# A longer hold for urgent work in a static instruction plan, and a later start of the second half's attention

## The chip, the cores and the metric

One core of one Trainium2 chip. The metric is the device time of one execution in microseconds (us). A kernel is profiled in one execution and timed in several. Times are given as the median of the runs. A ratio is the mean time of one kernel's runs over the mean of the other's runs of the same rounds, so it is not quite the ratio of the medians that I quote.

## The reference, cut to what matters

```python
h  = x + A(_layernorm(x))          # A: x @ wqkv, phi = where(t>0, t+1, exp(t)) + 1e-6,
                                   #    linear attention (kv = phi(k)^T v, o = phi(q) kv / den), @ wo
h2 = h + B(_layernorm(h))          # B: relu(x @ W_gate) * (x @ W_up) @ W_down
# x is 1 x 2048 x 1024 bf16; 32 heads of 32; W_gate, W_up 1024 x 3584, W_down 3584 x 1024
```

Up to about 210 us the core works on A and on the two layernorms. The rest is B, a stream of large matmuls.

## The kernel before

The program is written as calls in a natural order. A `Plan` records each call as a node with an engine, a length (`hold`), a latency, its predecessors and a latest start (`late`). It then lists them once, at build time, in one fixed order for each engine, and issues that. So the order of every engine's queue is the plan's decision, made with the plan's idea of how long things take. The chip then follows the order whatever the true lengths are.

Some words for the calls. The large matmuls are done by 2 x 2 blocks with seven *products* in place of eight, so VectorE forms *sums* (or differences) of blocks of weights or of activations beforehand, and adds the products up afterwards. A *clamp* and a *join* make phi (min with 1, then max with 0 and add); a *residual add* adds x to a product; a *group* is a part of B's weights. In the views, `mem` is the on-chip memory SBUF, `psum` the one that TensorE's products land in, which the program divides into banks, and `tiny` is one or a few numbers per row.

The plan's lengths (cut):

```python
def cost(self, eng, op, out, ins, k):
    ...
    if eng == "vector":
        narrow = all(self.nbytes(a) == 2 and a.space != PSUM for a in (out, *ins) if self.free(a) > 1)
        mode = {"tensor_tensor": 2, "tensor_scalar": 4, "memset": 2}.get(op, 1) if narrow else 1
        ...
        return n / (0.96 * mode) + 69 + acc, 95 + self.SEM
    if eng == "scalar":
        return n / 1.2 + (51 if psum else 93) + 2 * acc, 105 + self.SEM
    return n * 1.15 + 100, 60 + self.SEM            # gpsimd
```

The choice of the next node (cut): of what is ready on the engine that is free first, the node with the earliest `late`. If a clearly more urgent node of that engine is ready within half of the chosen node's length, the engine holds for it.

```python
s, e, a = best                                      # time, engine, its available nodes
now = [i for i in a if nodes[i].ready <= s]
i = min(now, key=lambda i: (nodes[i].nom if e == "tensor" else nodes[i].late, i))
v = nodes[i]
if e != "tensor":
    soon = [j for j in a if s < nodes[j].ready < s + 0.5 * v.hold and nodes[j].late < v.late - 1500.0]
    if soon:
        i = min(soon, key=lambda j: (nodes[j].late, j))
        v = nodes[i]
        s = v.ready
v.start = s
clock[e] = s + v.hold
```

The normalise of a layernorm (x times 1/std minus mean) runs on GpSimd, and so does a tiny negation of the mean:

```python
def finish(self, on_dve=False):
    self.rstd_()                                    # two tiny ScalarE activations
    xn = self.xn
    (nc.vector if on_dve else nc.gpsimd).tensor_scalar(out=xn, in0=self.x, scalar1=self.negm[:], scalar2=self.rstd[:], ...)
    nc.sync.dma_start_transpose(out=XI[self.i][:, :, self.r:self.r + P], in_=xn)
```

The second half's attention (token blocks 8 to 15; `nd01`, `nd2` are numerator and denominator, then `wo`) is put into a queue of units, one of which is taken at each tick between matmul groups:

```python
t8, t9 = tiles[NTS:NTS + 2]
tick.units.extend([t8.nd01, None, t9.nd01, None, t8.nd2, t9.nd2] + steps(NTS, 2 * NTS, 2, 0, False)[4:])
```

## Time and profile before

| | before |
|---|---|
| median of 3 runs | 727.81 us (727.63 to 728.01) |
| profiled run | 726.09 us, span 724.3 us |
| TensorE busy | 99% of the span |
| VectorE, ScalarE, GpSimd busy | 78%, 38%, 11% |

TensorE is nearly always busy, so the kernel can only gain where TensorE pauses. In this document **a pause is the distance between the starts of two matmuls less the pace of the first** (215.6 ns for 512 columns), worked out from the start times in the trace. That is some 0.16 us more than the idle time that a timeline line shows, as the ends of matmuls overlap the next starts. The prediction shows the lines and how they are read.

### The profile page before, as it was taken

The numbers are of one execution on the slowest core, as the hardware profiler recorded it, in microseconds if no ns is written. First come the engines' busy times: TensorE is split into PE (matmuls) and PEld (weight loads), VectorE is DVE, ScalarE is ACT, GpSimd is POOL, SyncE is SP. The second block draws the span as 40 slices with busy tenths as digits, with TensorE's granted clock in tenths as the row PEclk, the third lists the DMA queues.
The fourth block names the chain that finished last, engine by engine and source line by source line (L and its number), as shares of the span: only waits on it lengthen the run. The fifth ranks groups of instructions, "written<-read, shape, count | busy, mean of one in ns | idle before, by whom it ended". The sixth has DMA issues, their size and how long they took to land.

```text
span 724.3 us, 11221 instructions
## 1 busy us (share of the span) xinstructions
PE 714.4 (99%) x4163; PEld 396.7 (55%) x4163; DVE 563.9 (78%) x954; ACT 277.3 (38%) x540; POOL 77.8 (11%) x88
## 2 busy tenths in 40 slices
PE   8999999999999999999999999999999999999998
PEld 4444545444444444444444444444444688888887
DVE  7897745887796885666767968769758879899996
ACT  5877555666554443333333333333333220001100
POOL 1342000002202110000000000000000004001452
PEclk9999999999999999999999999999999999999999
DMA  9556406069766630446145575685681878777974
GB/s 300 165 117 110 138 0 212 23 109 216 160 156 151 140 73 6 129 136 186 60 139 188 165 244 157 202 253 186 198 262 51 276 265 209 216 265 238 242 80 60
DMA packets 156503, 117.40 MB, mean 162 GB/s; under 512 B 54944, under 2 KB 140192, under 8 KB 156320
## 3 DMA queue, kind: packets, MB, share of 16 engines
q1 hardware_dynamic: 148832, 113.01, 53.9%
q0 software_dynamic: 7616, 3.67, 4.8%
q8 instruction: 32, 0.52, 0.3%
q14 instruction: 23, 0.19, 0.1%
HBM read 70.52 MB, written 34.08 MB: 144 GB/s over the span
## 4 chain that ended last, share of the span: by engine, by line
PE 85%; DVE 2%; DMA 2%; ACT 1%; issue 0%; POOL 0%; ACTq 0%
PE psum L122 85%; DVE mem L122 2%; DMA mem<-mem 2%; ACT mem L122 1%; POOL mem L122 0%; ACT tiny L122 0%; DVE tiny L122 0%; ACTq L122 0%
## 5 line engine op out<-in xcount | busy, mean ns | idle before, releaser
L122 PE MATMUL psum<-mem 128*128 128x512 f16 (+4 forms) x4147 | 713.3, 334 | 6.5 <-ACT mem L122 2.7
L122 PEld LDWEIGHTS <-mem 128*128 128x128 f16 (+1 forms) x4163 | 396.7, 98 | 323.8 <-issue 8.0
L122 DVE TENSOR_TENSOR mem<-psum,mem 128x512 f32<-128x512 f32 (+2 forms) x240 | 187.4, 794 | 99.3 <-ACT mem L122 65.1
L122 DVE TENSOR_TENSOR mem<-mem 128x512 f16<-128x512 bf16 (+8 forms) x400 | 241.6, 643 | 14.9 <-DMA mem<-mem 9.6
L122 ACT COPY mem<-psum 128x512 f32<-128x512 f32 (+2 forms) x124 | 92.7, 749 | 209.4 <-PE psum L122 197.9
L122 ACT COPY psum<-psum 128x512 f32<-128x512 f32 (+1 forms) x68 | 49.1, 722 | 160.3 <-PE psum L122 147.6
L122 POOL DMA_DIRECT2D out_dram<-mem x28 | 34.1, 1299 | 413.8 <-DVE mem L122 413.7
L122 ACT ACTIVATE mem<-psum 128x512 bf16<-128x512 f32 x90 | 53.6, 598 | 18.5 <-PE psum L122 18.0
L122 DVE SCALAR_TENSOR_TENSOR mem<-mem 128x512 bf16<-128x512 bf16 (+1 forms) x71 | 57.7, 813 | 1.3
L122 POOL TENSOR_SCALAR mem<-mem,tiny 128x1024 bf16<-128x1024 bf16 x28 | 37.5, 1338 | 196.9 <-ACT tiny L122 176.8
L122 DVE SCALAR_TENSOR_TENSOR mem<-psum,mem 128x512 bf16<-128x512 f32 x66 | 45.4, 688 | 11.9 <-PE psum L122 7.9
L122 ACT ACTIVATE mem<-mem,tiny 128x1024 bf16<-128x1024 bf16 x24 | 27.4, 1143 | 11.0 <-DVE tiny L122 5.8
L122 DVE TENSOR_SCALAR mem<-mem 128x512 bf16<-128x512 bf16 (+1 forms) x49 | 16.3, 332 | 17.6 <-ACT mem L122 17.4
L122 DVE TENSOR_TENSOR mem<-psum,tiny 128x384 bf16<-128x384 f32 (+1 forms) x48 | 22.9, 508 | 5.3 <-ACT tiny L122 3.9
L122 ACT ACTIVATE mem<-mem 128x1024 bf16<-128x1024 f32 (+1 forms) x23 | 24.3, 1056 | 6.5 <-DVE mem L122 6.4
L122 ACT ACTIVATE tiny<-tiny 128x1 f32<-128x1 f32 (+2 forms) x112 | 22.8, 206 | 7.5 <-DVE tiny L122 4.7
L122 ACT ACTIVATE tiny<-psum 128x12 f32<-128x12 f32 (+1 forms) x48 | 8.1, 169 | 13.9 <-PE psum L122 13.4
L122 DVE BATCH_NORM_STATS2 tiny<-mem 128x6 f32<-128x512 bf16 x16 | 10.2, 682 | 2.5 <-DMA mem<-in_A_x_dram 2.5
L122 ACT CAST mem<-psum 128x512 bf16<-128x512 f32 x18 | 10.4, 582 | 4.2 <-PE psum L122 3.7
L122 POOL TENSOR_SCALAR tiny<-tiny 128x1 f32<-128x1 f32 x14 | 4.7, 337 | 25.2 <-ACT mem L122 13.3
L122 ACT ACTIVATION_READ_ACCUMULATOR mem<-mem,tiny 128x1 f32 x24 | 4.5, 188 | 0.0
L122 DVE TENSOR_SCALAR tiny<-tiny 128x1 f32<-128x1 f32 x16 | 3.4, 210 | 0.3
(18 smaller groups left out, 14.4 us busy)
## 6 DMA issues: line engine op xcount, KB each, us to landing
l_dram<-mem SPq DMA_DIRECT2D x98, 128.0 KB, 2.2
mem<-l_dram SPq DMA_DIRECT2D x12, 896.0 KB, 6.4
mem<-in_A_x_dram SPq DMA_DIRECT2D x32, 256.0 KB, 3.0
mem<-in_B_W_up_dram SPq DMA_DIRECT2D x14, 512.0 KB, 5.3
mem<-in_B_W_gate_dram SPq DMA_DIRECT2D x14, 512.0 KB, 4.3
mem<-in_B_W_down_dram SPq DMA_DIRECT2D x28, 256.0 KB, 3.4
r_dram<-mem SPq DMA_DIRECT2D x56, 128.0 KB, 1.8
mem<-r_dram SPq DMA_DIRECT2D x8, 896.0 KB, 5.0
```

The source lines that it names most:

```text
L122: call = lambda: getattr(getattr(self.nc, eng), op)(*args, **k)
```

## The change

The intent: let the engines other than TensorE, VectorE and ScalarE above all, wait up to 1.2 lengths of the less urgent node, not 0.5, for an urgent one that is nearly ready, during the first 215 us of the plan, where TensorE's pauses are. And let the second half's attention start four ticks later, so that it meets the last projection less tightly.

```diff
+    SHORT = 215000.0
...
-                soon = [j for j in a if s < nodes[j].ready < s + 0.5 * v.hold and nodes[j].late < v.late - 1500.0]
+                wait = (1.2 if s < self.SHORT else 0.5) * v.hold
+                soon = [j for j in a if s < nodes[j].ready < s + wait and nodes[j].late < v.late - 1500.0]
...
-    tick.units.extend([t8.nd01, None, t9.nd01, None, t8.nd2, t9.nd2] + steps(NTS, 2 * NTS, 2, 0, False)[4:])
+    tick.units.extend([None] * 4 + [t8.nd01, None, t9.nd01, None, t8.nd2, t9.nd2] + steps(NTS, 2 * NTS, 2, 0, False)[4:])
```

## The prediction

> **What bounds the kernel now.** I read the page first, then the busy time of the engines by stretch, then each idle spot of TensorE in the timeline, and last the orders in which the two programs issue their instructions (an order has no times in it).
>
> ```profile
> PE 714.4 (99%) x4163; PEld 396.7 (55%) x4163; DVE 563.9 (78%) x954; ACT 277.3 (38%) x540; POOL 77.8 (11%) x88
> ```
>
> TensorE is busy for 99% of the span at full clock. Busy does not mean fast here, as matmul ends are modelled, so I checked the pace: from 300 to 400 us, a stretch of 128x512 matmuls, the table by stretch counts 465 in 100 us, 215 ns each. So after the attention the kernel is a full TensorE stream, and the change can only win what TensorE loses by waiting. Where it waits, by stretch (busy us and count of PE, PEld, DVE, ACT, POOL, then clock, DMA share, GB/s):
>
> ```profile
> 20.00:60.00 40.00, 38.83 (x203) 18.33 (x201) 34.40 (x68) 33.67 (x73) 16.76 (x19) 1.00 0.56 132
> 60.00:140.00 80.00, 79.65 (x437) 38.77 (x436) 52.07 (x89) 46.26 (x81) 3.94 (x5) 1.00 0.37 99
> 140.00:152.00 12.00, 11.16 (x67) 5.53 (x66) 11.76 (x24) 7.56 (x25) 0.00 (x0) 1.00 0.24 45
> 152.00:186.00 34.00, 34.00 (x190) 16.75 (x189) 26.16 (x66) 20.41 (x66) 8.71 (x7) 1.00 0.92 187
> 186.00:210.00 24.00, 21.82 (x117) 10.26 (x116) 20.62 (x41) 16.22 (x41) 1.36 (x2) 1.00 0.65 166
> 210.00:280.00 70.00, 70.00 (x355) 32.98 (x354) 55.09 (x113) 30.49 (x88) 9.81 (x8) 1.00 0.48 105
> 280.00:720.00 440.00, 440.00 (x2715) 265.48 (x2713) 348.40 (x532) 112.14 (x146) 34.07 (x28) 1.00 0.62 181
> ```
>
> Idle is 1.17 + 0.35 + 0.84 + 2.18 = 4.54 us, all before 210 us. An idle spot costs more than it shows: a 512-column matmul lasts 381 ns on average but starts follow at 215 ns, so a stream overlaps by 0.16 us that a pause loses too. From the matmul starts, the pauses of over 0.2 us sum to some 6.7 us. **That is the whole prize, 0.9% of 727.81 us**: 2% faster is out of reach.
>
> **What the Trainium skill says.** "VectorE: DVE Perf Modes", section "The TRN2 errata", gives 215 ns for an N=512 matmul; the trace agrees, so nothing is hidden in the busy stretches. "PSUM — Partial Sum Buffer", section "Engine vs sequencer instructions", says the ScalarE and VectorE queues are strict FIFO: an instruction that waits holds all behind it. The lines at 187.93 us below agree. "Perfetto Trace Analysis", section "Optimizing Scalar/DVE Operations", gives some 93 ns of overhead for ScalarE on SBUF and twice that for the profiled latency; the 128x1 activations here take 206 ns (page), while the kernel's plan books 1/1.2 + 93 = 94 ns. "DMA: Bandwidth & Descriptors", section "Two DMAs through the same engine are not ordered", says that descriptors of one queue start in order; no line of this trace shows that by itself, but I use it below for a transpose that changes places with a load.
>
> **The change part by part.** No work is added or removed: 4163 matmuls and the same instructions stand in both programs. (1) Before the plan's time of 215 us, VectorE and ScalarE may idle up to 1.2 (not 0.5) of an instruction's length for a more urgent one. (2) The second half's attention starts four units later. By the orders, VectorE has 368 of 921 entries at another place, ScalarE 189 of 507, and the TensorE order is the same up to 137 us. I followed each pause through the new order with durations of the old trace.
>
> Part one at 193 us, the largest pause. VectorE, then ScalarE:
>
> ```profile
> 187.93 0.42 DVE L122 TENSOR_TENSOR mem<-mem 128x512 f16<-128x512 bf16 x1 [2.76 <-DMA mem<-mem]
> 188.27 0.68 DVE L122 SCALAR_TENSOR_TENSOR mem<-psum,mem 128x512 bf16<-128x512 f32 x1
> ...
> 187.86 0.58 ACT L122 COPY mem<-psum 128x512 f32<-128x512 f32 x1 [2.99 <-PE psum L122]
> 189.60 1.06 ACT L122 ACTIVATE mem<-mem 128x1024 bf16<-128x1024 f32 x1 [1.15 <-DVE mem L122]
> 190.56 1.14 ACT L122 ACTIVATE mem<-mem,tiny 128x1024 bf16<-128x1024 bf16 x1
> ...
> 192.17 0.57 ACT L122 COPY mem<-psum 128x512 f32<-128x512 f32 x1
> ...
> 192.79 1.46 PE L122 MATMUL psum<-mem 128*128 128x512 bf16 x6 [1.46 <-ACT mem L122]
> ```
>
> A sum waits 2.76 us for a transpose and holds up the residual add behind it (its product was done at 186.1); the add then sets the start of two 1.1 us activations, and those stand before the copy that TensorE waits for (its input was ready at 190.4). In the new order the residual add comes before the sum, the long exp after the copy: add 186.1 to 186.8, its mean to 187.0, the square 188.45 to 189.6, two tiny ones to 190.0, an exp of 0.58 to 190.55, the copy to 191.1. TensorE gets there at 191.1. **-1.6 us.**
>
> At 147 to 151 us the chain of waits is a transpose of 3.12 us:
>
> ```profile
> 147.48 3.12 DMA mem<-mem
> 150.59 0.05 issue
> 150.64 1.47 PE psum L122 x6
> ```
>
> In the new order a 0.68 us sum no longer stands before the last product join, nor a 0.28 us clamp before the scaling that feeds the transpose. The transpose is issued 0.2 + 0.28 earlier, and two pauses of 0.2 just before shrink. **-0.5 us**; the transpose itself stays.
>
> At 29 and 55 us, in the opening:
>
> ```profile
> 20.50 6.22 DVE L122 TENSOR_TENSOR mem<-mem 128x512 f16<-128x512 bf16 x8 [0.37 <-DMA mem<-mem]
> ...
> 26.64 1.28 DVE L122 BATCH_NORM_STATS2 tiny<-mem 128x6 f32<-128x512 bf16 x2
> ...
> 28.02 0.69 DVE L122 TENSOR_TENSOR mem<-psum,mem 128x512 f32<-128x512 f32 x1
> ...
> 28.76 2.53 PE L122 MATMUL psum<-mem 128*128 128x512 bf16 x11 [0.54 <-DVE mem L122]
> ```
>
> TensorE waits (0.70 with the overlap) for the add at 28.02, which stood behind 1.28 us of statistics. The new order moves the statistics behind it. But it also lets VectorE hold, from about 18.1, for the transpose that landed at 20.48, and does one weight difference (1.22 us) and a clamp and join (1.0) after that wait, not before. So -1.28 + 2.2: about 0.9 us later. One relief: SyncE now issues that transpose before a 256 KB load, so it may land up to 0.9 us earlier (an estimate: 256 KB at the 303 GB/s of the first 20 us), but that load, which ScalarE needs at 20.2, then comes later. I take **+0.5 us** here. At 55 us (0.73 lost) the copy stood behind two tiny activations waiting for statistics; the new order puts them elsewhere: **-0.5**. At 68 us two more tiny activations of 0.2 come before the copy: +0.2. At 76 us an add passes a 1.22 us join: -0.2. The pause of 0.3 at 128 us has the same order in both: 0.
>
> Part two, 200 to 209 us: pauses of 0.72, 0.28 and 0.24 us, where attention pieces meet the ends of the last projection. Their matmuls now stand six to seven products of 0.86 us later, so the join they wait for is done. But the same vector work (3 scalings, joins, sums; DVE is busy 20.6 of 24 us) then meets the next products, and I find new waits of 0.1 to 0.7 us when I follow it. **-0.4.** The last transposes of that attention end some 3.5 us later; the first matmul that needs them comes 16 us after (263.0 against 279.0), so nothing is lost there.
>
> Sum: -1.6 - 0.5 + 0.5 - 0.5 + 0.2 - 0.2 - 0.4 = **-2.5 us**, 725.3 us.
>
> **The rivals.** (a) *Holding costs more than it saves*: the plan's times are too short (94 ns for 206; a transpose that lands 5.2 us after issue at 15.25 us, where it books 3.6), so holds last longer than meant. For it: VectorE is at 34.4 of 40 us from 20 to 60. Against it: only the hold at 18 us is near a pause; the later background work has 7 us and more to spare (a sum's end to its first matmul). If the opening loses 1.0 and the 55 us pause stays: 726.5 to 727.5. (b) *The stall only moves*: at 193 us TensorE comes earlier to the same congested vector work, and the gain is given back by 209 us: 726.5. (c) *Everything clears*: opening -0.7, all pauses to 209 gone: -6 us, 722. It would need the plan to be exact; the 3.1 us transpose alone forbids it.
>
> **Range and chances.** All three lie within 6 us. I predict 725.3 us, 723.3 to 727.6 at 8 in 10; wider upward, as (a) and (b) can come together. Faster by 2% would be 713.3, more than all pauses; slower by 2% needs 14.6 us of new ones. So within 2% is nearly sure.
>
> **What would show it.** Right: PE idle from 186 to 200 falls from about 1.5 to near 0 with VectorE no longer idle for a DMA at 185 to 188; 140 to 152 keeps one DMA pause of 0.3 to 0.6; 280 to 720 stays full with equal counts; the pause at 28.8 stays or grows, with a VectorE idle of 1.5 to 2.4 us just before 20.5. Wrong: no VectorE idle there and no pause at 29 (then nearer 724), or new PE pauses of over 1 us between 195 and 215 or in 210 to 280 (then 727 and more).

## The result, and the profile after

| | before | after |
|---|---|---|
| median of 5 runs each | 727.81 us (727.06 to 728.07) | 726.63 us (726.26 to 726.87) |
| ratio | | 0.9987 (95% interval 0.9973 to 1.0000) |
| profiled run | 726.09 us | 726.87 us |

The change gained about 1.2 us, 0.13%: the same within 2%. The interval ends at no gain (1.0000), and that of the repeat below just beyond it (1.0005); but none of the ten timed runs of the changed kernel (at most 727.02 us) is as slow as the fastest of the 14 runs of before in their rounds (727.04). The two *profiled* runs stand the other way round. The profile of before is the fastest of all its runs, the profile of after one of the slowest of the changed kernel. So before reading a difference into the two traces I needed to know which pauses belong to the order and which to the run.

The page of the changed kernel, engines and the GpSimd normalise (columns of the second line: count, busy us, mean ns, idle before and its cause):

```profile
PE 711.2 (98%) x4112; PEld 396.7 (55%) x4163; DVE 566.3 (78%) x954; ACT 277.3 (38%) x540; POOL 81.6 (11%) x88
...
L123 POOL TENSOR_SCALAR mem<-mem,tiny 128x1024 bf16<-128x1024 bf16 x28 | 40.8, 1459 | 181.7 <-ACT tiny L123 168.9
```

TensorE's row has 4112 of 4163 matmuls: 51 records are missing, so its busy time is too low, and the table by stretch below can't be set against that of before. All weight loads are there, and from them I filled in the starts. The second line is the first hint: the same 28 normalises took 1459 ns on average. Before, the row said:

```profile
L122 POOL TENSOR_SCALAR mem<-mem,tiny 128x1024 bf16<-128x1024 bf16 x28 | 37.5, 1338 | 196.9 <-ACT tiny L122 176.8
```

The changed kernel's busy time by stretch (PE, PEld, DVE, ACT, POOL, then clock, DMA share, GB/s):

```profile
20.00:60.00 40.00, 36.49 (x189) 17.45 (x192) 32.61 (x58) 30.45 (x67) 16.69 (x16) 1.00 0.49 120
...
140.00:152.00 12.00, 11.60 (x69) 5.76 (x68) 11.05 (x21) 8.97 (x27) 0.00 (x0) 1.00 0.12 23
152.00:186.00 34.00, 32.80 (x178) 16.08 (x183) 29.45 (x69) 18.77 (x63) 7.18 (x6) 1.00 0.86 180
186.00:210.00 24.00, 23.66 (x119) 11.07 (x120) 20.70 (x42) 16.49 (x38) 2.39 (x2) 1.00 0.75 173
```

186 to 210 us is now nearly full. 20 to 60 us lost 3.5 us of busy time (before: 1.2), and 152 to 186 us, full before, now has holes. Some of that is missing records, but the pauses say the same. Sums of TensorE's pauses in us by stretch; the second profile of each kernel comes from the experiments:

| stretch, us | before, 1st profile | before, 2nd | after, 1st | after, 2nd |
|---|---|---|---|---|
| 0 to 20 | 2.91 | 3.47 | 3.67 | 3.04 |
| 20 to 40 | 0.74 | 0.59 | 1.62 | 1.67 |
| 40 to 60 | 1.10 | 2.00 | 2.07 | 2.11 |
| 60 to 80 | 0.74 | 1.26 | 0.18 | 0.18 |
| 120 to 160 | 1.78 | 1.80 | 1.31 | 1.30 |
| 160 to 180 | 0.05 | 0.05 | 1.28 | 1.27 |
| 180 to 220 | 3.03 | 3.59 | 0.72 | 0.76 |
| 240 to 280 | 0.00 | 0.00 | 0.22 | 0.22 |

The stretch that the change was made for is mended. The timeline of the changed kernel there, VectorE, then ScalarE, then TensorE:

```profile
188.94 0.69 DVE L123 SCALAR_TENSOR_TENSOR mem<-psum,mem 128x512 bf16<-128x512 f32 x1 [0.89 <-PE psum L123]
...
190.71 1.55 DVE L123 TENSOR_TENSOR mem<-mem 128x512 f16<-128x512 bf16 x4 [0.21 <-DMA mem<-mem]
...
190.67 0.59 ACT L123 COPY mem<-psum 128x512 f32<-128x512 f32 x1 [2.59 <-PE psum L123]
191.15 1.15 ACT L123 ACTIVATE mem<-mem,tiny 128x1024 bf16<-128x1024 bf16 x1
...
193.26 0.59 ACT L123 COPY mem<-psum 128x512 f32<-128x512 f32 x1
...
185.72 22.29 PE L123 MATMUL psum<-mem 128*128 128x512 bf16 x110
208.24 4.00 PE L123 MATMUL psum<-mem 128*128 128x512 f16 x25 [0.23 <-ACT psum L123]
```

The residual add (188.94) now stands before the sums that wait for the transpose (190.71), the long exp is gone from ahead of the copy at 193.26, and the timeline shows TensorE from 185.72 to 208 us in one piece (a pause of 0.16 us by the starts) where it stopped for 1.46 us at 192.79 before. Between 140 and 160 us the two small pauses are gone and the transpose stays: 3.12 us in the chain of waits, to the same hundredth as before.

```profile
149.08 3.12 DMA mem<-mem
```

What was gained there was lost in three other places. First, the opening. VectorE holds for a transpose (2.23 us idle) and then does nine sums with a clamp and a join among them, so that the add which TensorE needs comes late:

```profile
20.55 3.49 DVE L123 TENSOR_TENSOR mem<-mem 128x512 f16<-128x512 bf16 x5 [2.23 <-DMA mem<-mem]
...
24.90 4.66 DVE L123 TENSOR_TENSOR mem<-mem 128x2048 f16<-128x2048 bf16 x4
...
29.68 0.68 DVE L123 TENSOR_TENSOR mem<-psum,mem 128x512 f32<-128x512 f32 x1
...
30.41 25.34 PE L123 MATMUL psum<-mem 128*128 128x512 bf16 x137 [1.42 <-DVE mem L123]
```

(A merged row names the shape of its first instruction: two of the five sums are of 128x2048, one of the four is of 128x512.) One of the four in the second line, of 128x2048, takes 2.06 us, at 27.50; a sum of that shape takes 1.22 us elsewhere. Second, at 57 us (GpSimd, VectorE, ScalarE, TensorE):

```profile
50.51 4.33 POOL L123 TENSOR_SCALAR mem<-mem,tiny 128x1024 bf16<-128x1024 bf16 x2
54.81 0.20 POOL L123 TENSOR_SCALAR tiny<-tiny 128x1 f32<-128x1 f32 x1
...
50.50 1.26 DVE L123 SCALAR_TENSOR_TENSOR mem<-mem 128x1024 bf16<-128x1024 f32 x1
...
55.05 1.15 ACT L123 ACTIVATE mem<-mem,tiny 128x1024 bf16<-128x1024 bf16 x1 [1.90 <-POOL tiny L123]
...
57.63 2.53 PE L123 MATMUL psum<-mem 128*128 128x512 f16 x11 [1.88 <-ACT mem L123]
```

Two normalises, 1.19 us each when undisturbed, take 4.33 us. The tiny negation behind them, whose input was ready at 52.69, runs at 54.81. ScalarE's square waits 1.90 us for it, and behind the square stands the copy that TensorE waits for. With two normalises of 1.19 us the negation would have started some 1.9 us earlier, about as long as TensorE's pause (2.04 us); that is worked out from the trace, and no run isolates it. Third, at 166 to 177 us, where before had no pause at all (VectorE, GpSimd, TensorE):

```profile
165.00 1.16 DVE L123 TENSOR_TENSOR mem<-mem 128x1024 f16<-128x1024 bf16 x1
166.08 0.68 DVE L123 SCALAR_TENSOR_TENSOR mem<-psum,mem 128x512 bf16<-128x512 f32 x1
...
164.42 1.20 POOL L123 TENSOR_SCALAR mem<-mem,tiny 128x1024 bf16<-128x1024 bf16 x1 [3.84 <-ACT tiny L123]
...
172.11 4.95 PE L123 MATMUL psum<-mem 128*128 128x512 bf16 x27 [0.35 <-DVE mem L123]
```

The hold moved four weight sums of group 0 from 137 to 152 us to between the attention's steps. Three of them stand just before a residual add (as at 166.08) that frees a PSUM bank for TensorE. Each of the three takes 1.15 us; the same sums took 0.68 us before, and the fourth, at 178.33, takes 0.68 still. The three pauses are 0.22, 0.51 and 0.51 us.

All three places have one thing in common: a VectorE instruction with two inputs in SBUF beside a GpSimd normalise, one of which is too long. The Trainium skill has it, and my prediction had not looked: "SBUF — State Buffer", section "Who interferes with whom", says that a VectorE instruction with two SBUF inputs, or in one of its two-port fast modes, and a GpSimd instruction that reads SBUF contend for a pair of ports that the two engines share, that it is an exclusive lock, and that the later one blocks. The traces agree: GpSimd's first normalise at 50.51 us took 2.49 us, 1.30 more than undisturbed, and the VectorE instruction with two SBUF inputs that starts beside it lasts 1.26 us. (A sum of 0.41 us, at 51.68, also lies within it and is not stretched, so this is no exact account.) The plan has no such thing in `cost` or `schedule`.

### The profile page after: what moved, and what is told of

It reads as the page before. It is cut to its first block, busy times and chain, and to the rows that moved or that the text cites. A ratio compares the mean times of both kernels' runs of the same rounds, so it can differ in the third digit from the quotient of the medians.

```text
span 725.1 us, 11180 instructions
## 1 busy us (share of the span) xinstructions
PE 711.2 (98%) x4112; PEld 396.7 (55%) x4163; DVE 566.3 (78%) x954; ACT 277.3 (38%) x540; POOL 81.6 (11%) x88
## 3 DMA queue, kind: packets, MB, share of 16 engines
q0 software_dynamic: 7616, 3.67, 4.9%
## 4 chain that ended last, share of the span: by engine, by line
PE 88%; ACT 2%; DVE 1%; issue 1%; DMA 0%; POOL 0%; ACTq 0%; DVEq 0%
PE psum L123 88%; ACT mem L123 1%; DVE mem L123 1%; DMA mem<-mem 0%; ACT tiny L123 0%; ACT psum L123 0%; DVE tiny L123 0%; POOL tiny L123 0%; ACTq L123 0%; DVEq L123 0%
## 5 line engine op out<-in xcount | busy, mean ns | idle before, releaser
L123 PE MATMUL psum<-mem 128*128 128x512 bf16 (+4 forms) x4096 | 710.3, 334 | 10.3 <-ACT mem L123 2.6
L123 POOL TENSOR_SCALAR mem<-mem,tiny 128x1024 bf16<-128x1024 bf16 x28 | 40.8, 1459 | 181.7 <-ACT tiny L123 168.9
```

The source lines that it names most:

```text
L123: call = lambda: getattr(getattr(self.nc, eng), op)(*args, **k)
```

## The experiments

Every kernel was timed in five rounds against the kernel before on the same chip, except where said. The chip was another for each of four groups (the four runs up to "only from 80 us on"; the four up to "told of the shared pair"; the next three; the last corner), so medians of different groups are compared with care. "After" stays the name of the changed kernel.

### The changed kernel again

Its diff is a comment.

> The changed kernel once more, byte for byte but for a comment. It measures how far one profile and one median stray. If the two profiles of before and after were a fair pair, this profile's TensorE pauses agree with the first profile of the changed kernel within 0.3 us in each 20 us stretch, except the opening's wait for the first weights (0.2 us before, 0.9 after, same order in both kernels, so put down to the transfer). The median is expected at 726.6, between 726.2 and 727.2, against 727.8 for the kernel before.

Measured: 726.83 us (726.32 to 727.02) against 727.53, ratio 0.9991 (0.9978 to 1.0005). From 20 us on, the pauses agree with the first profile within 0.06 us in each stretch (last column of the table above). In the first 20 us they differ by 0.63 us, 0.43 of it at the wait for the first weights (0.88 and 0.45). So these traces repeat to a few hundredths after 20 us, and the opening varies from run to run.

### The hold alone, and the later start alone

```diff
-    tick.units.extend([None] * 4 + [t8.nd01, ...      # e1: the hold alone
+    tick.units.extend([t8.nd01, ...
-                wait = (1.2 if s < self.SHORT else 0.5) * v.hold      # e2: the later start alone
+                wait = 0.5 * v.hold
```

> The longer hold alone; the second half's attention begins where it did. Theory (the hold's losses are its own: 29 us +0.9, 57 us +1.3, 166 to 177 us +1.2; its gains 42 to 76 us -0.9, 193 us -0.9 as ScalarE keeps the order of before there, 150 us -0.4; nothing is won at 200 to 209 us): sum +1.2, so 728.5 to 729.5, slower than both. Rival (the hold gives all the gain, the later start nothing): 726.6 as the changed kernel.

Measured: 727.91 us (727.58 to 728.49), ratio 1.0006 (0.9993 to 1.0018). The pauses are those of after up to 180 us (1.55, 2.06, 0.18, 1.31 and 1.27 us in the stretches of the table), and 0.37 us is left at 194 us. The ones at 204, 207 and 213 us (0.72, 0.28, 0.55) are back. The hold's losses are its own, as the theory said, and they eat up what it wins. The time was 0.6 us less than the theory's least, most likely because I had reckoned from before's first profile, with its lucky 55 us pause.

> The later start alone; holds of half an instruction as before. Theory: the opening up to 130 us is as before (pauses at 29 us 0.7, at 55 us 0.7, none at 166 to 177 us); 200 to 209 us wins 0.9; at 193 us VectorE still has the sum that waits for a transpose ahead of the residual add, so most of 1.6 us stays there. About 726.9, and 725.5 if the later start takes the 193 us pause as well. Rival (the gain is the hold's): 727.8 as before.

Measured: 727.06 us (726.57 to 727.80), ratio 0.9994 (0.9982 to 1.0007). 200 to 220 us fell from 1.40 to 0.38 us; 193 us kept its pause (1.48 at 191.81 and 0.52 at 194.05). So neither part gains anything that these intervals can show, and each wins pauses that the other does not. The later start has a small loss of its own: 0.20 us at 270 us, here and in the changed kernel, not with the hold alone. There TensorE waits for an addition that stands behind a sum of 1.52 us (0.68 undisturbed) beside a normalise, in the changed kernel at 268.00. One thing was not as expected: the pause at 55 us was 1.61, not 0.73 us, though up to about 178 us this kernel has before's order on every engine.

### The hold only from 80 us on

```diff
-                wait = (1.2 if s < self.SHORT else 0.5) * v.hold
+                wait = (1.2 if 80000.0 < s < self.SHORT else 0.5) * v.hold
```

> Both parts, but the longer hold only from 80 to 215 us of plan time; TensorE's order is that of the changed kernel throughout, the other engines' too from 98 us. Theory (the opening's losses at 29 and 57 us come from the holds of the opening): pauses there fall back to 0.7 and 0.7, those at 42, 68 and 76 us come back (0.3, 0.25, 0.4 together), so some 1.3 us faster than the changed kernel: 725.3. 166 to 177 us keeps its three pauses of 1.2 us in all. Rival (the profile's opening is chance, or the stall moves on): 726.6 as the changed kernel.

Measured: 726.08 us (725.97 to 726.35), ratio 0.9981 (0.9968 to 0.9993), 0.75 us less than after in the same rounds. The pause at 29 us fell to 0.49, and the three at 166 to 177 us stayed (1.23), as expected. But the pause at 55 us was again 1.6 us:

```profile
56.54 3.83 PE L123 MATMUL psum<-mem 128*128 128x512 f16 x17 [1.45 <-ACT mem L123]
```

So the size expected was wrong by the 55 us pause, and the question was what it is in the kernel before itself.

### The kernel before again

A single look (state unknown, as one run has no comparison), for a second profile. Its diff is a comment.

> The kernel before once more, for a second profile. In the first one GpSimd's normalise at 51.99 us took 1.48 us and VectorE's sum of 128x512 beside it (52.16) 0.42; in the two kernels run since that keep this order, the normalise took 1.20 and the sum 1.30, with the same offset of 0.17 us between their starts, and TensorE paused 1.6 us, not 0.7, at that place. Theory: the two race for the port pair that VectorE and GpSimd share, and the first profile showed the rarer outcome; so here the pause at 55 us is 1.6 us and the time is 726.9 to 727.9. Rival: the outcome belongs to the order of the whole program; then 0.7 us here as in the first profile, and about 726.1.

Measured: 728.49 us (above the range expected), and the pause at 55 us is 1.62 us. The two profiles of the same program, first one and second one, GpSimd's normalise and VectorE's sum beside it:

```profile
51.99 1.48 POOL L122 TENSOR_SCALAR mem<-mem,tiny 128x1024 bf16<-128x1024 bf16 x1 [2.55 <-issue]
...
52.16 0.42 DVE L122 TENSOR_TENSOR mem<-mem 128x512 f16<-128x512 bf16 x1
```

```profile
52.43 1.19 POOL L122 TENSOR_SCALAR mem<-mem,tiny 128x1024 bf16<-128x1024 bf16 x1 [2.54 <-issue]
...
52.59 1.30 DVE L122 TENSOR_TENSOR mem<-mem 128x512 f16<-128x512 bf16 x1
```

In the first, VectorE's sum took 0.42 us and GpSimd paid 0.29 us. In the second, GpSimd was undisturbed and the sum took 1.30. Their starts are 0.17 and 0.16 us apart: the trace can't tell the two cases apart beforehand, only afterwards. The sum is followed on VectorE by statistics, a clamp and a join, and ScalarE's copy waits on tiny activations behind the statistics; so the 0.88 us reach TensorE whole (0.73 to 1.62). Five profiles hold this order at this place (the two of before, and three kernels with the opening's order of before); four show 1.6 us, one 0.73. **The first profile of before, on which the prediction rests, showed the outcome that no other of the five has.** The second is also worse at 78 and 195 us (0.73 and 2.17 us, not 0.22 and 1.62), so the timed median lies between the two profiles.

### GpSimd's normalises shortened, all orders kept

The result is wrong: four normalises write 64 of 1024 columns, while the plan books the full length, so that every engine's order is that of after. (The comparison with the reference does not notice these columns.)

```diff
+            w = 64 if nc.last() in (707, 740, 773, 805) else D
-            nc.gpsimd.tensor_scalar(out=self.hn, in0=self.h, ...)
+            nc.gpsimd.tensor_scalar(out=self.hn[:, 0:w], in0=self.h[:, 0:w], ...)
+            nc.nodes[-1].hold = D * 1.15 + 100
```

> The changed kernel, every engine's order untouched, but GpSimd's four normalises between 159 and 176 us write 64 of 1024 columns (the plan still books the full length, so the result is wrong on purpose). Theory: the three pauses of TensorE at 166.8, 172.1 and 177.4 us (1.24 us in all) come from VectorE's sums with two inputs in SBUF, which wait for the port pair that GpSimd holds: 1.15 us each beside a normalise, 0.68 without. Then the sums take 0.68 us, the pauses sum to under 0.3 us, and the time is 725.3 to 725.7. Rival (the sums are simply in the way of the residual adds, 0.68 us of VectorE work before each): pauses stay at 0.4 us and more each, 726.6.

Measured: 725.83 us (725.10 to 726.14), ratio 0.9976 (0.9963 to 0.9988). The same sum as shown above at 165.00, and the normalise, now of 64 columns:

```profile
165.25 0.68 DVE L123 TENSOR_TENSOR mem<-mem 128x1024 f16<-128x1024 bf16 x1
...
164.73 0.39 POOL L123 TENSOR_SCALAR mem<-mem,tiny 128x64 bf16<-128x64 bf16 x1 [4.77 <-ACT tiny L123]
```

The sum takes 0.68 us, the three pauses are gone (160 to 180 us: 0.05, not 1.27), and no other stretch after 20 us changed by more than 0.05 us. The sums stand where they stood; only the neighbour is shorter. The rival, that the sums are simply in the way, falls. The time, just above the range expected, fell 0.8 to 1.0 us below after's two medians, not the whole 1.2; the opening of this profile was the 0.2 to 0.8 us longer one.

### The hold only from 180 us on

```diff
-                wait = (1.2 if s < self.SHORT else 0.5) * v.hold
+                wait = (1.2 if 180000.0 < s < self.SHORT else 0.5) * v.hold
```

> Both parts, but the longer hold only from 180 to 215 us of plan time. The opening and 80 to 180 us then have the order of before: the weight sums stand at 137 to 152 us again. Theory: no pauses at 166 to 177 us (-1.24 against the run with the hold from 80 us on), the pauses at 146 to 151 us come back (+0.48), 193 and 200 to 209 us stay won: 725.3, the best so far. Rival (the hold gains everywhere after 80 us): 726.1 or more.

Measured: 725.21 us (724.40 to 726.51), ratio 0.9967 (0.9954 to 0.9981). The pauses of 166 to 177 us are gone, those of 146 to 151 us are back (1.34), 193 us stays won (0.16). Against the run with the hold from 80 us on (726.08), the two terms make -1.23 + 0.44 = -0.8; the medians differ by 0.9, but the two ran in different rounds. This profile, of the slowest of the five runs, also has a pause of 0.62 us at 79 us. Four profiles have before's order up to there, and they show 0.22, 0.73, 0.0 and 0.62 us at that place; the cause is not known.

### The plan is told of the shared pair

Nothing else is changed: both parts stand, with the long hold everywhere up to 215 us. Only the building of the order is different; no instruction is added.

```diff
+    def shares(self, eng, op, out, ins):
+        inner = [a for a in ins if a.space != PSUM and self.free(a) > 1]
+        if eng == "gpsimd":
+            return op != "dma_start" and bool(inner)
+        if eng != "vector" or not inner:
+            return False
+        narrow = op == "tensor_scalar" and all(self.nbytes(a) == 2 and a.space != PSUM for a in (out, *inner))
+        return len(inner) > 1 or narrow
...
+        ready = lambda i: max(nodes[i].ready, pair) if nodes[i].pair else nodes[i].ready
...                                                  # ready(i) takes the place of nodes[i].ready in the choice
             v.start = s
+            if v.pair:
+                pair = s + v.hold
```

> The changed kernel with the longer hold everywhere up to 215 us, but the plan knows of the shared port pair: VectorE instructions with two SBUF inputs, VectorE's narrow fast ones and GpSimd's with an SBUF input are booked one at a time. Theory: the holds did harm only because the plan did not see this conflict, so with it the pauses at 57 us and at 166 to 177 us shrink to under 0.8 and under 0.3 us, and 29 us to 0.8: 724.5 to 725.5. Rival (holds harm the opening whatever the plan knows, as the transposes land late): 726 to 727.

Measured: 723.32 us (722.99 to 723.88), ratio 0.9945 (0.9932 to 0.9957): 4.1 us less than before. The pause at 57 us is 0.38 us, those at 166 to 177 us are gone (the plan moved the sums to 175 us and later, away from the normalises), and 60 to 140 us lost its small ones. 29 us did not improve: the pause is 1.59 us, and the sum of 2.06 us is still there. The time is 1.2 us under the least expected. So what the theory foretold came at two of the three places, and at the third the plan could not prevent the meeting; there the run below shows that the hold brings the loss. A count supports the theory: over the first 280 us, VectorE's sums with two SBUF inputs were lengthened by 5.2 us in all in the changed kernel, and by 1.1 here (2.4 and 3.3 in the two profiles of before), counted against 0.42, 0.68 and 1.22 us undisturbed for 512, 1024 and 2048 columns. GpSimd's normalises were lengthened by 7.3 us in the changed kernel and by 5.3 here (4.0 and 3.6 before). But this run also has another order: at 57 us one normalise is still stretched (2.27 us, at 50.97) and the square stands elsewhere, so the pair and the order are not told apart at that place. Only at 166 to 177 us does a run with all orders kept show the cause.

### The pair known, the hold only from 30 us on

```diff
-                wait = (1.2 if s < self.SHORT else 0.5) * v.hold      # on top of the run above
+                wait = (1.2 if 30000.0 < s < self.SHORT else 0.5) * v.hold
```

> The plan that knows of the shared pair, both parts of the change, but the longer hold only from 30 us on. Theory: in the opening's first stretch the hold at 17 us is a loss by itself, as VectorE then does its background sums after the transpose and one of them meets GpSimd's normalise (2.06 us, not 1.22); without it the pause at 29 us falls from 1.6 to 0.5 to 0.7, the pause near 57 us stays under 0.5 and 193 us stays won: 722.2 to 722.8, the best so far. Rival (the other order from 26 to 78 us brings the 57 us pause of 1.6 back): 723.5 to 724.

Measured: 722.20 us (722.00 to 722.60), ratio 0.9928 (0.9916 to 0.9941). **This beats both kernels**, by 5.4 us and, against after's two medians, by 4.4 to 4.6. From 29 us on, the timeline shows TensorE for 31 us without a break, where between 40 and 60 us alone it lost 1.1 to 2.1 us before and after:

```profile
29.09 31.09 PE L132 MATMUL psum<-mem 128*128 128x512 bf16 x171 [0.55 <-DVE mem L132]
```

After 20 us, 3.2 us of pauses are left (7.6 and 9.5 in the two profiles of before): 0.72 at 29, the transpose's 0.76 at 149, 0.72 at 203 us, and small ones.

### The other corners: what the two parts are worth under the right plan

The pair known, with neither part (the hold stays at 0.5); with the later start alone; with the hold from 30 us alone.

```diff
+                wait = 0.5 * v.hold                       # e8, on the kernel before with the pair
-                wait = (1.2 if s < self.SHORT else 0.5) * v.hold      # e9, on after with the pair
+                wait = 0.5 * v.hold
-    tick.units.extend([None] * 4 + [t8.nd01, ...      # e10, on the run above
+    tick.units.extend([t8.nd01, ...
```

> The kernel before, neither part of the change, with the plan that knows of the shared pair. Theory: the opening wins what the pair costs there (57 us: 1.6 to under 0.5), the rest stays: 193 us 1.6 to 2.2, 146 to 151 us 1.3, 200 to 209 us 1.2. About 726.2 against 727.5. Rival (the pair explains all, the change is worth nothing once the plan is right): 723.3, as the run with both.

> The plan that knows of the shared pair and the later start, holds of half an instruction. Theory: 29 us 0.7 (won against the run with holds, -0.9), 146 to 151 us 1.3 (+0.4), at 193 us 1.5 to 2.0 in all as in the run with the later start alone (+1.7), 204 us won (-0.5): about 724.0. So the longer hold is worth 1.5 us or more once it is kept out of the opening. Rival (a right plan finds the order at 193 us by itself): 722.5 or less.

> The plan that knows of the shared pair and the longer hold from 30 us on, without the later start: the fourth corner of the square (neither part 725.45, later start alone 725.58, both 722.20). Up to 180 us every order is that of the run with both parts, so pauses there are equal (29 us 0.7, 150 us 0.75). Theory (each part needs the other around 200 us): pauses at 204 to 214 us of 1.2 to 1.7 us come back, about 0.4 at 194 us as in the run with the hold alone: 723.2 to 724.0. Rival (the hold is worth all of it): 722.2.

| pair known to the plan | no later start | later start |
|---|---|---|
| hold 0.5 | 725.45 (724.86 to 726.46) | 725.58 (725.28 to 726.60) |
| hold 1.2 from 30 us | 723.14 (722.58 to 723.49) | 722.20 (722.00 to 722.60) |

The plan that knows the pair is about 2.1 us faster with no other change. The hold is then worth 2.3 to 3.4 us. The later start gives about 0.9 with the hold (those two runs are of different groups, and their intervals against before, 0.9916 to 0.9941 and 0.9926 to 0.9953, overlap) and nothing that shows without it. Two expectations missed. With neither part, the 193 us pause was gone (180 to 200 us: 0.0 us), and 2.0 us of pauses stood at 202 to 207 us instead, so the stall had moved; the pause at 57 us came down to 0.74 only. Nor was that the plan's doing as far as the trace tells, for the sum still starts 0.17 us after the normalise, and won this time:

```profile
53.35 0.75 DVE L131 TENSOR_TENSOR mem<-mem 128x512 f16<-128x512 bf16 x2
...
53.51 1.57 POOL L131 TENSOR_SCALAR mem<-mem,tiny 128x1024 bf16<-128x1024 bf16 x1 [2.54 <-issue]
```

(VectorE's row starts with a sum at 53.35 and ends with one at 53.68; GpSimd is at 53.51. With the later start alone it is the same: 0.75 us of pause, a normalise of 1.58.) So the 2.1 us may hold some luck in that race. And with the later start alone, 193 us kept 1.36 us and the small pauses of the opening stayed, 725.58 where I expected 724.0: here the rival, that a right plan finds the good order by itself, is refuted for that stretch. The last corner came in just under the expected range (723.14), with 0.37, 0.72 and 0.28 us at 189, 199 and 202 us.

As a check on the method: over all kernels, the pauses after 20 us and the medians go together. 3.24 us of pauses stand beside 722.20, 3.88 beside 723.14, 4.40 beside 723.32, 6.71 beside 726.08, 7.6 beside 726.63 and 8.63 beside 727.91. Over all eleven kernels other than before the difference is 718.4 to 719.4 us. By this, before's median of 727.5 to 727.8 stands for some 8.5 us of pauses (an estimate from those pairs), between its two profiles.

## Why the prediction was right, and which steps of it were not

It said 725.3 us, between 723.3 and 727.6, and the median was 726.63. Total and verdict hold, the total in part by luck: against the profile that the prediction read, the terms as they came out sum to nothing (-0.06 us, below), and the gain of 1.2 us is there because that profile was faster than the kernel's timed runs. Of the sum's terms, two hold (193 and 147 to 151 us), those at 29 and at 200 to 209 us were mis-sized, that at 68 us had the wrong sign, one failed (55 us), and one large and two small ones were missing.

- **193 us, -1.6: right**, in mechanism and size. The add stands ahead of the sums, the exp behind the copy. The pause went from 1.62 (2.17 in the second profile) to 0.16. With the later start alone it stays, so it is the hold's gain, though the hold alone leaves 0.37.
- **147 to 151 us, -0.5: right.** The stretch from 120 to 160 us went from 1.78 to 1.31, with the transpose of 3.12 us unchanged.
- **68 and 76 us, +0.2 and -0.2: better than said.** I looked for two tiny activations in the way and an add that passes a join. Of the pauses of 0.25, 0.23 and 0.22 us one of 0.14 is left: -0.6.
- **29 us, +0.5: two pieces of the mechanism right, a third missing, the size short by 0.4.** The working had the order, about +0.9, and a transpose that lands earlier, for which I took about half. From VectorE's start on the transposed data to the add's start is 7.52 us before (20.50 to 28.02) and 9.13 after (20.55 to 29.68), +1.61. Of this 0.84 is the sum at 27.50 that met GpSimd's normalise, and 0.77 the order. The earlier landing came, nearly whole: counted from the matmul that waits for the first weights (9.93 and 10.70 us), 10.57 us in before and 9.85 in after. So +0.77 and -0.72 nearly cancel, and what is left of the +0.88 is, by this reckoning, the port pair, which was not in the sum. Without the hold in the first 30 us the pause is 0.5 to 0.7 again.
- **55 us, -0.5: the step that failed.** "The new order puts them elsewhere": it does put the two tiny activations elsewhere, but ScalarE now waits for a negation behind two GpSimd normalises that the pair had stretched from 2.4 to 4.33 us. The pause is 2.04 to 2.08 us, where the first profile of before had 0.73 and the second 1.62. So it is +1.3 against the profile I read, and +0.4 against the outcome seen in four profiles of five. That the stretch makes the pause is read from the trace, as said above; no run with the orders kept tests it here.
- **200 to 209 us, -0.4: right in kind, half the size.** 1.40 to 0.54 and 0.58, -0.85.
- **Missing terms.** At 41 to 42 us two small pauses went, -0.3. At 270 us one of +0.2 came with the later start, where I had said that nothing is lost. The large one is 166 to 177 us, +1.2. I said that the later background work has time to spare. That holds for the sums' own deadlines. What I did not ask is what they stand in front of at the new place, and beside what.

The sum of the terms over 20 to 280 us, against the first profile of before, is -0.06 us (7.62 to 7.56). Against the second it is -1.9. The measured -1.2 and, in the later rounds, -0.7 lie between. That before's own spread comes from such a race is read from the two traces for the 55 us pause. For the differences at 78 and 195 us it stays open, and so does what sets the opening's wait for the first weights (2.9 to 4.6 us in the first 20 us, over all profiles).

Of the rivals, (a), holding costs more than it saves, came true in its two places and in its time (726.5 to 727.5), but not for its reason: I blamed plan times that are too short, and a hold that lasts too long. The shortened normalises show at 166 to 177 us, and the plan with the pair makes likely at 57 us, that it is the company the held-back work ends up in. At 29 us about half of the loss is the order itself (0.77 of 1.61 us). What I named as the sign of the thing going wrong, new pauses of over 1 us between 195 and 215 us, did not come; the new ones came at 166 us, where I had not looked. Rival (b), the stall only moves, did not come: 180 to 220 us went from 3.03 to 0.72 us. Rival (c), everything clears, failed at the opening, which lost where it was to gain.

## What to carry to other kernels

When a scheduler or a reorder moves work on VectorE or GpSimd, check what it will run *beside*, not only what it will run before: here VectorE's sums with two SBUF inputs took up to three times as long next to a GpSimd normalise (1.30 for 0.42 us), and a static plan that doesn't know it can put them there. In this kernel a hold for urgent work paid where a chain was late and nothing heavy waited behind it (193 us), and cost where it pushed a block of background work in front of the next urgent instruction (29 and 166 us), so restrict it by measurement. And take two profiles of the kernel before you trust a pause of under a microsecond: one place where two engines meet made 0.9 us here, with the same program.

## What the Trainium skill lacked or had wrong

- "SBUF — State Buffer" says that whichever of the two starts first gets the pair. With start records 0.16 to 0.17 us apart, GpSimd first in all five profiles of that order, the sum of 128x512 won once (0.42 us, normalise 1.48) and lost four times (1.30, normalise 1.19); under the plan that knows the pair it won at 0.17 us too (0.42, normalise 1.57). So the order of the starts in the records doesn't tell which of the two gets the lock, and the page doesn't say how to read it.
- The same page gives the rule but no durations for these shapes. The runs show 1.15 for 0.68 us (sum of 128x1024), 2.06 for 1.22 (128x2048), 1.30 for 0.42 (128x512), and 2.49 for 1.19 (normalise of 128x1024 on GpSimd).
- No page that I read says that such a lock makes the time of an unchanged program fall into two outcomes: 0.73 or 1.62 us of pause at one place in five profiles with the same order there.
